# Chunk attention and a token mixer on one core: quarter-array transposes, a shared PSUM ring and an end ordered by hand

## The chip, the cores and the metric

One NeuronCore of a Trainium2 chip runs the kernel. The metric is the device time of one execution in microseconds. The kernel before has a median of 155.53 us over 3 runs (155.32 to 157.15).

## What is computed

q, k and v are float32 of shape (8 batches, 8 heads, 576 rows, 64). Attention runs inside chunks of 64 rows, then the heads are laid side by side to x of shape (8, 576, 512), and a token mixer follows:

```python
# attention, per batch, head and chunk of 64 rows
scores = q_c @ k_c.T / 8
attn   = softmax(scores)
x      = attn @ v_c                      # then (B, S, H*D) = (8, 576, 512)
# token mixer, per batch
wq, wk = x @ w_q, x @ w_k                # 576 x 64 each
W_tok  = wq @ wk.T / 8                   # 576 x 576, never formed in the kernel
out    = relu(W_tok @ x) @ w_out         # 576 x 512
```

The kernel computes `wq @ (wk.T @ x)`: the 64x512 product in the middle is its `g`.

## The kernel before

**Attention** is cut into 36 units (NU), each of 16 chunks; a batch is 4.5 units. One unit passes through these steps:

- `stage_a1`: TensorE transposes q and k, 16 transposes per unit. Each takes 128 rows by 64 columns of `qn` as weights and the 128x128 identity as moving operand, and writes 64 partitions by 128 columns of `tp` (one PSUM bank, one buffer). The array is split into two halves of 64 columns.
- `stage_a2`: VectorE copies all of `tp` (128x1024, float16) to `qkt` in SBUF.
- `stage_b1`: 16 products of 64x64 give the scores `sp`, VectorE takes the row maximum `mx`.
- `stage_b2`: VectorE subtracts (`sh`), ScalarE exponentiates (`es`).
- `stage_c`: four 128x128 transposes of `es` into `ep`, which has a PSUM bank of its own; ScalarE copies it to `et`.
- `stage_d1`, `stage_d2`: 16 products of 64x65 with v (a column of ones gives the denominator) into `xp` (two banks), then on VectorE `den`, `rec` and the normalised `x_nat`.

**The mixer** of a batch is a chain of steps, each with PSUM tiles from one ring of three banks (`m_psum`, tag "m"): `p_xt` (three times: six transposes `tx`, copy to `xt`), `p_wqk` in two halves (`wpa` of 512 and `wpb` of 64 columns, accumulated over four weights; copies to `wqkT`; then a VectorE copy of its lower 64 partitions to the upper 64 of `wqd`, line 178), `p_wkn` (18 transposes of 64x64), `p_g`, `p_mixed` twice and `p_mixed_tail` (products `ma` and `mb`, relu on ScalarE to `rmx` and `rt`), then four `p_out` (four 512-column products into `op`, copy to `osb`, store) and for each pair of batches a `p_out_tail`. A batch takes 17.5 tiles of the ring: 3 `tx`, 2 for `p_wqk`, `wknp`, `gp`, 4 `ma`, 2 `mb`, 4.5 for the outputs.

**The order** is written by hand: every engine executes its instructions in the order in which the Python code issues them. The loop over `kk` issues, per iteration: `stage_b1(kk)`, `stage_d1(kk-2)`, the mixer steps planned for place 0, `stage_a1(kk+2)`, `stage_c(kk-1)`, `stage_b2(kk)`, `stage_d2(kk-2)`, `stage_a2(kk+2)`, then the mixer steps of place 2 and as many `p_out` as a budget allows. So VectorE's order per unit is `mx`, `sh`, `den`, `rec`, `x_nat`, `qkt`; TensorE's is `sp`, `xp`, a mixer step, `tp`, `ep`, then `tx`, `wpa`/`wpb` or `op`. What is left after the loop is merged by a rule with estimated costs (lines 514 to 527). Loads are issued by GpSimd, output stores by SyncE.

Of the kernel before, what the change touches and what calls it, by code (L numbers as in the profile page):

```python
# [17 lines left out]
def kernel(  # L18
# [15 lines left out]
    nc = tc.nc  # L34
# [10 lines left out]
    NU = B * NI // 8  # L45
    R, G = 2, 32
# [12 lines left out]
    osb_pool = ctx.enter_context(tc.tile_pool(name="osb", bufs=4))  # L59

    PS = bass.MemoryType.PSUM
    t_psum = ctx.enter_context(tc.tile_pool(name="tps", bufs=1, space=PS))
    s_psum = ctx.enter_context(tc.tile_pool(name="sps", bufs=1, space=PS))
    et_psum = ctx.enter_context(tc.tile_pool(name="etps", bufs=1, space=PS))
    x_psum = ctx.enter_context(tc.tile_pool(name="xps", bufs=1, space=PS))
# [60 lines left out]

    def relu(on_vector, to, of):
        if on_vector:
            nc.vector.tensor_scalar(to, of, scale_moe, 0.0, op0=ALU.mult, op1=ALU.max)
        else:  # L130
            nc.scalar.activation(to, of, AF.Relu, scale=scale_moe)  # L131
# [3 lines left out]
    def make_moe(b):  # L135
        st = sts[b]

        def p_xt(g):
            def run():
                if g == 0:  # L140
                    st["xt"] = xt_pool.tile([P, NI, CH], F16, name="xt", tag="xt")
                xt = st["xt"].rearrange("p (s two) c -> p s (two c)", two=2)
                tx = m_psum.tile([P, 6, P], F16, name="tx", tag="m")
                for j in range(6):
                    nc.tensor.transpose(  # L145
                        tx[:, j, :], x_nat[:, b * NS + 6 * g + j, :, :], ident[:]
                    )
                if b == B - 1 and g == 2:
                    nc.vector.tensor_copy(xt[:, 12:15, :], tx[:, 0:3])
                    nc.scalar.copy(xt[:, 15:18, :], tx[:, 3:6])  # L150
                else:
                    nc.scalar.copy(xt[:, 6 * g : 6 * g + 6, :], tx[:])  # L152

            return run

        def p_wqk(half):
            def run():
                xt = st["xt"]
                if half == 0:
                    st["pa"] = m_psum.tile([P, 512], F32, name="wpa", tag="m")  # L160
                    st["pb"] = m_psum.tile([P, CH], F32, name="wpb", tag="m")
                pa, pb = st["pa"], st["pb"]
                for i in (2 * half, 2 * half + 1):
                    flags = dict(start=(i == 0), stop=(i == HQ - 1))
                    nc.tensor.matmul(
                        pa[:, :], lhsT=wqk16[:, i, :], rhs=xt[:, NC_ * i : NC_ * i + 8, :], **flags
                    )
                    nc.tensor.matmul(
                        pb[:, :], lhsT=wqk16[:, i, :], rhs=xt[:, NC_ * i + 8, :], **flags
                    )  # L170
                if half == 0:
                    return
                wqkT = moe_pool.tile([P, S], F16, name="wqkT", tag="wqkT")
                wqd = moe_pool.tile([P, S], F16, name="wqd", tag="wqd")
                nc.scalar.copy(wqkT[:, 0:512], pa[:])
                (nc.vector.tensor_copy if b == B - 1 else nc.scalar.copy)(wqkT[:, 512:S], pb[:])

                nc.vector.tensor_copy(wqd[CH:P, :], wqkT[0:CH, :])
                st["wqkT"], st["wqd"] = wqkT, wqd

            return run

        def p_wkn():


            wk = st["wqkT"][CH:P]
            wp = m_psum.tile([P, NC_, DH], F16, name="wknp", tag="m")
            for n in range(NC_):
                for o in range(2):
                    nc.tensor.transpose(  # L190
                        wp[CH * o : CH * o + CH, n, :],
                        wk[:, ds((2 * n + o) % NC_ * CH, CH)],
                        ident[CH:P, CH:P],
                    )
            wkn = moe_pool.tile([P, NC_, DH], F16, name="wkn", tag="wkn")
            nc.scalar.copy(wkn[:], wp[:])
            st["wkn"] = wkn

        def p_g():


            wkn = st["wkn"]
            gp = m_psum.tile([P, 2, P], F32, name="gp", tag="m")
# [29 lines left out]
        def p_mixed(w):  # L233
            def run():
                if w == 0:
                    st["rmx"] = moe_pool.tile([P, HQ, 512], F16, name="rmx", tag="rmx")
                ms = [m_psum.tile([P, 512], F32, name=f"ma{par}", tag="m") for par in range(2)]
                mix(ms, w, slice(0, 512))
                for par in range(2):

                    relu(
                        b == B - 1 and par == 1,
                        st["rmx"][:, 2 * w + par].rearrange("p (c g r) -> p c g r", g=G, r=R),
                        ms[par][:].rearrange("p (c r g) -> p c g r", g=G, r=R),
                    )

            return run

        def p_mixed_tail():
# [5 lines left out]
            mb = [m_psum.tile([P, 2, CH], F32, name=f"mb{par}", tag="m") for par in range(2)]  # L255
# [3 lines left out]
            for par in range(2):  # L259
                relu(  # L260
                    b == B - 1 and par == 1,
# [4 lines left out]
        def p_out(t):  # L266
            def run():
                rmx = st["rmx"]
                op = m_psum.tile([P, DM], F32, name="op", tag="m")
# [8 lines left out]
                osb = osb_pool.tile([P, DM], F32, name="osb", tag="osb")  # L278
                if b == B - 1 and t == 3:

                    hw = DM // 2
                    nc.scalar.copy(osb[:, 0:hw], op[:, 0:hw])
                    nc.vector.tensor_copy(osb[:, hw:], op[:, hw:])
                    nc.scalar.dma_start(out[b, ds(t * P, P), 0:hw], osb[:, 0:hw])
                    nc.sync.dma_start(out[b, ds(t * P, P), hw:], osb[:, hw:])
                    return
                (nc.vector.tensor_copy if b == B - 1 and t % 2 else nc.scalar.copy)(osb[:], op[:])  # L287
# [4 lines left out]
        def p_out_tail():  # L292

            rt = st["rt"]
            op = m_psum.tile([P, DM], F32, name="opt", tag="m")
# [9 lines left out]
            nc.scalar.copy(osb[:], op[:])  # L305
# [26 lines left out]
    def stage_a1(u):  # L332

        tp = t_psum.tile([P, 2, 2, 4, R, G], F16, name="tp", tag="tp")
        for j in range(2):
            b, t = batch_of(2 * u + j)
            for ti in range(2):
                part = t >= cuts[1][0]
                src = data[b, part, ti][:, :, t - cuts[part][0]]
                for r in range(R):  # L340
                    for sl in range(2):
                        nc.tensor.transpose(  # L342
                            tp[CH * sl : CH * sl + CH, j, ti, :, r, :],
                            src[:, sl, r * D : r * D + D],
                            ident[:],
                        )
        state[u] = {"tp": tp}

    def stage_a2(u):
# [3 lines left out]
            qkt[:].rearrange("p j t c k -> p (j t c k)"),  # L353
            tp[:].rearrange("p j t c r g -> p (j t c r g)"),
# [37 lines left out]
    def stage_c(u):  # L392
        es = state[u]["es"]
        ep = et_psum.tile([P, 4, P], F16, name="ep", tag="ep")
# [97 lines left out]
    for kk in range(NU + 2):  # L492
        if kk < NU:
            stage_b1(kk)
# [7 lines left out]
        if 1 <= kk <= NU:  # L502
            stage_c(kk - 1)
        if kk < NU:
            stage_b2(kk)
# [8 lines left out]
    rest = [x for key in sorted(plan) for x in plan[key]]  # L514
    last = [x for x in rest if x[0] == B - 1]
    rest = [x for x in rest if x[0] < B - 1]
    clock, due = 0.0, 0.0
    while last or rest or outs:
        if last and (clock >= due + last[0][2] or not (rest or outs)):
            entry = last.pop(0)  # L520
            clock = due = max(clock, due) + run(entry)
        elif rest:
            clock += run(rest.pop(0))
        else:
            _, cost, step = outs.pop(0)
            step()
            clock += cost
# [28 lines left out]
```

## Time and profile before

| | |
|---|---|
| median of 3 runs | 155.53 us |
| the profiled execution's own time | 156.93 us |
| its span, first to last instruction | 155.0 us |
| VectorE in 20 to 40 us, 40 to 60, 60 to 80, 80 to 100 | 18.86, 19.18, 18.43, 18.73 us busy of 20 |
| TensorE in the same stretches | 15.90, 17.72, 19.25, 19.52 us |
| ScalarE in the same stretches | 11.17, 16.20, 17.43, 17.62 us |
| GpSimd's last load issued | at 103.2 us |
| last `sp` starts, last TensorE product ends | 121.43 us, about 150.0 us |

An execution's own time holds the span and about 1.9 us around it. In a row of a group of instructions, the number before the bar's second part is the sum of their durations and the mean of one; because products follow each other in a pipeline, a mean duration is longer than the distance between two starts, and it is the distance that sets a stretch's length. "busy" of TensorE counts the modelled ends, so a busy engine may still stand and wait for a bank.

### The profile page before, as it was taken

How to read it: one execution, taken by the hardware profiler on the slowest of the kernel's cores; microseconds unless marked ns; L12 is line 12 of the kernel's file. 1: busy time of each engine (PE TensorE's matmuls, PEld its weight loads, DVE VectorE, ACT ScalarE, POOL GpSimd, SP SyncE). 2: the span in 40 equal slices, each digit the busy share in tenths (PEclk: the TensorE clock that was granted, in tenths of full speed). 3: DMA queues.
4: the chain of work that ended last, by engine and by line, in shares of the span. 5: the costliest groups of instructions: out<-in, count | busy, mean ns of one | idle time of the engine just before them, and what ended most of it. 6: DMA issues, size and time to landing. Idle time of an engine off the chain costs nothing.

```text
span 155.0 us, 6022 instructions
## 1 busy us (share of the span) xinstructions
PE 129.1 (83%) x2576; PEld 84.1 (54%) x2576; DVE 111.3 (72%) x231; ACT 105.9 (68%) x208; POOL 94.4 (61%) x140
## 2 busy tenths in 40 slices
PE   0266989759588999999999999999999898898870
PEld 0145768557465666666567467565666453442320
DVE  0056799999999999998989999989897942013020
ACT  3004144656589889886997998699889998556430
POOL 8999999999799799688789988880000000000000
PEclk9999999999999999999999999999999999699997
DMA  2999999999999999999999999999224315035383
GB/s 23 146 156 164 155 167 166 111 135 156 165 167 175 164 174 174 212 211 209 196 229 182 206 211 225 193 241 219 50 72 97 117 65 189 33 111 144 139 268 136
DMA packets 82570, 24.64 MB, mean 159 GB/s; under 512 B 77296, under 2 KB 78064, under 8 KB 82544
## 3 DMA queue, kind: packets, MB, share of 16 engines
q0 software_dynamic: 77152, 14.82, 114.6%
q1 hardware_dynamic: 5248, 9.31, 17.4%
q8 instruction: 20, 0.33, 0.8%
q10 hardware_dynamic: 144, 0.13, 0.3%
q14 instruction: 6, 0.05, 0.1%
HBM read 29.62 MB, written 9.44 MB: 252 GB/s over the span
## 4 chain that ended last, share of the span: by engine, by line
PE 45%; DVE 22%; ACT 19%; issue 5%; DMA 4%; POOL 2%; SPq 1%; ACTq 0%; DVEq 0%; POOLq 0%
PE op L271 12%; PE tp L342 6%; ACT rmx L131 6%; DVE qkt L352 5%; DVE sh L381 5%; DVE x_nat L427 4%; DVE mx L375 4%; ACT es L389 4%; PE sp L367 4%; PE ep L396 4%; PE ma L227 3%; PE tx L145 3%; PE gp L212 3%; DMA qn<-in_k_dram 3%; ACT osb L287 2%
## 5 line engine op out<-in xcount | busy, mean ns | idle before, releaser
L101 POOL DMA_DIRECT2D vt<-in_v_dram x48 | 38.4, 855 | 4.1 <-DMA vt<-in_v_dram 2.6
L342 PE MATMUL tp<-ident,qn 128*64 128x128 f16 x576 | 27.4, 241 | 8.2 <-DMA qn<-in_q_dram 6.1
L398 ACT COPY et<-ep 128x512 f16<-128x512 f16 x36 | 21.2, 590 | 18.9 <-PE ep L396 18.9
L271 PE MATMUL op<-wout,rmx 128*128 128x512 f16 x128 | 32.1, 383 | 1.6 <-ACT osb L287 1.3
L352 DVE COPY qkt<-tp 128x1024 f16<-128x1024 f16 x36 | 24.5, 682 | 10.0 <-PE tp L342 9.9
L389 ACT ACTIVATE es<-sh 128x512 f16<-128x512 f32 x36 | 23.0, 638 | 10.7 <-DVE sh L381 9.9
L91 POOL DMA_DIRECT2D qn<-in_k_dram x32 | 26.7, 872 | 3.9 <-DMA qn<-in_k_dram 1.5
L342 PEld LDWEIGHTS <-qn 128*64 128x64 f16 x576 | 21.5, 122 | 12.4 <-DMA qn<-in_q_dram 6.5
L91 POOL DMA_DIRECT2D qn<-in_q_dram x32 | 27.5, 907 | 0.9 <-DMA qn<-in_q_dram 0.5
L375 DVE TENSOR_REDUCE mx<-sp 128x8 f32<-128x512 f32 x36 | 24.7, 686 | 3.6 <-PE sp L367 3.4
L381 DVE TENSOR_TENSOR sh<-sp,mx 128x512 f32<-128x512 f32 x36 | 24.9, 692 | 2.3
L427 DVE TENSOR_TENSOR x_nat<-xp,rec 128x512 f16<-128x512 f32 x36 | 24.9, 692 | 1.2
L287 ACT COPY osb<-op 128x512 f32<-128x512 f32 x30 | 17.7, 594 | 6.5 <-PE op L271 2.8
L367 PEld LDWEIGHTS <-qkt 64*64 64x64 f16 x576 | 12.9, 115 | 14.3 <-issue 6.3
L367 PE MATMUL sp<-qkt 64*64 64x64 f16 x576 | 17.1, 203 | 3.4 <-DVE qkt L352 1.9
L152 ACT COPY xt<-tx 128x768 f16<-128x768 f16 x23 | 18.4, 801 | 0.1
L271 PEld LDWEIGHTS <-rmx 128*128 128x128 f16 x128 | 11.7, 98 | 12.1 <-issue 2.5
L412 PE MATMUL xp<-vt,et 64*64 64x65 f16 x576 | 13.0, 201 | 4.8 <-DVE x_nat L427 4.1
L131 ACT ACTIVATE rmx<-ma 128x512 f16<-128x512 f32 x30 | 16.4, 596 | 0.4 <-PE ma L227 0.3
L396 PE MATMUL ep<-ident,es 128*128 128x128 f16 x144 | 15.2, 232 | 0.0
L412 PEld LDWEIGHTS <-et 64*64 64x64 f16 x576 | 9.6, 111 | 6.4 <-ACT es L389 3.8
L145 PE MATMUL tx<-ident,x_nat 128*128 128x128 f16 x144 | 12.7, 227 | 0.0
(47 smaller groups left out, 144.1 us busy)
## 6 DMA issues: line engine op xcount, KB each, us to landing
out_dram<-osb SPq DMA_DIRECT2D x31, 256.0 KB, 2.8
qn<-in_q_dram POOLq DMA_DIRECT2D x16, 160.0 KB, 5.5
qn<-in_k_dram POOLq DMA_DIRECT2D x16, 160.0 KB, 6.2
qn<-in_q_dram POOLq DMA_DIRECT2D x16, 128.0 KB, 6.1
qn<-in_k_dram POOLq DMA_DIRECT2D x16, 128.0 KB, 5.5
vt<-in_v_dram POOLq DMA_DIRECT2D x8, 160.0 KB, 6.5
vt<-in_v_dram POOLq DMA_DIRECT2D x16, 80.0 KB, 5.8
out_dram<-osb SPq DMA_DIRECT2D x9, 128.0 KB, 2.4
```

The lines of the kernel that those rows point to most:

```text
L91: nc.gpsimd.dma_start(tl[:, sl], of[sl, :, t0:t1, :])
L101: nc.gpsimd.dma_start(vt[to : to + rows, sl, :, 0:D], of[sl, at : at + rows, n0:n1, :])
L131: nc.scalar.activation(to, of, AF.Relu, scale=scale_moe)
L271: nc.tensor.matmul(op[:], lhsT=rmx[:, i, ds(t * P, P)], rhs=wout16[:, i, :], start=(i == 0), stop=(i == HQ - 1),)
L342: nc.tensor.transpose(tp[CH * sl : CH * sl + CH, j, ti, :, r, :], src[:, sl, r * D : r * D + D], ident[:],)
L352: nc.vector.tensor_copy(qkt[:].rearrange("p j t c k -> p (j t c k)"), tp[:].rearrange("p j t c r g -> p (j t c r g)"),)
L367: nc.tensor.matmul(sp[rows, i ^ sl, :], lhsT=qkt[rows, j, 0, c, :], rhs=qkt[rows, j, 1, c, :], start=True, stop=True,)
L375: nc.vector.tensor_reduce(mx[:], sp[:], axis=AX.X, op=ALU.max)
L381: nc.vector.tensor_tensor(out=sh[:].rearrange("p i (g r) -> p i r g", g=G, r=R), in0=sp[:].rearrange("p i (r g) -> p i r g", g=G, r=R), in ...
L389: nc.scalar.activation(es[:], sh[:], AF.Exp, scale=scale_attn)
L412: nc.tensor.matmul(xv[CH * par : CH * par + CH, sl, m, :], lhsT=et[at : at + CH, m, CH * sl : CH * sl + CH], rhs=vt[at : at + CH, sl, 0 : ...
L427: nc.vector.tensor_tensor(out=x_nat[:, 4 * u : 4 * u + 4, :, :].rearrange("p m l d -> p l m d"), in0=xv[:, :, :, 0:D], in1=rec[:, :, :, No ...
```

## The change

1. `stage_a1`: the 128-row transposes become 64x64 blocks, 32 per unit, each in one quarter of the array: `h` chooses the rows of the source (and of the array) and also one of two PSUM banks, `sl` the columns. `tp` now has two banks, each half used. `stage_a2` copies the same 1,024 elements, read from two banks and written in runs of 128.
2. `ep` loses its own bank. A helper `bank()` gives it, and every mixer tile, a bank of the ring of three: 22 tiles per batch instead of 17.5. After the switch `drain[0] = True` two of five tiles go to the banks of `sp` and `tp`.
3. `p_wqk`: 320 and 256 columns in place of 512 and 64. Before the drain, `wqd` is filled by a transfer on SyncE's queue (6 batches) and not by VectorE.
4. The last unit and the end are written out: `stage_c` and `stage_d` of the last two units are issued earlier among the mixer steps, `p_mixed_tail` of batch 5 later; copies are shared between ScalarE and VectorE (`copy(on_vector, ...)`), the last `tx`, `wknp` and `op` are cut in two, and `osb` has 8 buffers.

```diff
-    osb_pool = ctx.enter_context(tc.tile_pool(name="osb", bufs=4))
+    osb_pool = ctx.enter_context(tc.tile_pool(name="osb", bufs=8))
...
-    et_psum = ctx.enter_context(tc.tile_pool(name="etps", bufs=1, space=PS))
...
+    def bank(shape, dtype, name):
+        taken[0] += 1
+        if drained() and taken[0] % 5 == 0:
+            return s_psum.tile(shape, dtype, name=name, tag="sp")
+        if drained() and taken[0] % 5 == 2:
+            return t_psum.tile(shape, dtype, name=name, tag="tp")
+        return m_psum.tile(shape, dtype, name=name, tag="m")
...
-                nc.vector.tensor_copy(wqd[CH:P, :], wqkT[0:CH, :])
+                if drained():
+                    nc.vector.tensor_copy(wqd[CH:P, :], wqkT[0:CH, :])
+                else:
+                    nc.sync.dma_start(wqd[CH:P, :], wqkT[0:CH, :])
...
-        tp = t_psum.tile([P, 2, 2, 4, R, G], F16, name="tp", tag="tp")
+        tp = t_psum.tile([P, 2, 2, 2, 2, 2, R * G], F16, name="tp", tag="tp")
+        tq = tp[:, :, 0]
...
                 for r in range(R):
-                    for sl in range(2):
+                    for h, sl in ((0, 0), (1, 1), (0, 1), (1, 0)):
+                        rows = slice(CH * h, CH * h + CH)
                         nc.tensor.transpose(
-                            tp[CH * sl : CH * sl + CH, j, ti, :, r, :],
-                            src[:, sl, r * D : r * D + D],
-                            ident[:],
+                            tq[CH * sl : CH * sl + CH, h, j, ti, :, r * G : r * G + G],
+                            src[rows, sl, r * D : r * D + D],
+                            ident[rows, rows],
                         )
...
         nc.vector.tensor_copy(
-            qkt[:].rearrange("p j t c k -> p (j t c k)"),
-            tp[:].rearrange("p j t c r g -> p (j t c r g)"),
+            qkt[:].rearrange("p j t (h c) k -> p h (j t) (c k)", h=2),
+            tp[:, :, 0].rearrange("p h j t c k -> p h (j t) (c k)"),
         )
...
-        ep = et_psum.tile([P, 4, P], F16, name="ep", tag="ep")
+        ep = bank([P, 4, P], F16, name="ep")
...
-    while last or rest or outs:
...
+    u = NU - 1
+    stage_b1(u)
+    stage_d1(u - 2)
+    stage_c(u - 1)
+    stage_b2(u)
+    stage_d2(u - 2)
+    drain[0], taken[0] = True, 0
...
+    put(len(outs) - 14)
+    chain(B - 2, 2)
+    stage_c(u)
+    stage_d1(u - 1)
+    stage_d2(u - 1)
+    put()
+    stage_d1(u)
+    stage_d2(u)
+    chain(B - 1)
+    chain(B - 2)
+    chain(B - 1)
+    put()
+    chain(B - 1)
+    chain(B - 3)
+    chain(B - 2)
+    put(2)
+    chain(B - 1, 2)
+    chain(B - 2, 2)
+    chain(B - 1)
+    put()
+    chain(B - 1)
+    put()
+    chain(B - 2)
+    chain(B - 1, 3)
+    put(len(outs))
```

`chain(b)` issues the next mixer step of batch b (numbered from 0, so B - 1 is 7), `put(n)` the next n outputs.

More of the change, by code (lines that the diff above doesn't have):

```diff
@@ L45 @@
     NU = B * NI // 8
+    W0 = 5 * CH
     R, G = 2, 32
@@ L58 @@
     moe_pool = ctx.enter_context(tc.tile_pool(name="moep", bufs=2))
-    osb_pool = ctx.enter_context(tc.tile_pool(name="osb", bufs=4))
+    osb_pool = ctx.enter_context(tc.tile_pool(name="osb", bufs=8))
     PS = bass.MemoryType.PSUM
+    s_psum = ctx.enter_context(tc.tile_pool(name="sps", bufs=1, space=PS))
+    x_psum = ctx.enter_context(tc.tile_pool(name="xps", bufs=1, space=PS))
     t_psum = ctx.enter_context(tc.tile_pool(name="tps", bufs=1, space=PS))
-    s_psum = ctx.enter_context(tc.tile_pool(name="sps", bufs=1, space=PS))
-    et_psum = ctx.enter_context(tc.tile_pool(name="etps", bufs=1, space=PS))
-    x_psum = ctx.enter_context(tc.tile_pool(name="xps", bufs=1, space=PS))
     m_psum = ctx.enter_context(tc.tile_pool(name="mps", bufs=3, space=PS))
@@ L125, with drained, copy @@
     load_v(1, 0)
+    drain = [False]
+    taken = [0]
+    def bank(shape, dtype, name):
[5 more added lines that the diff above has]
+        return m_psum.tile(shape, dtype, name=name, tag="m")
+    def drained():
+        return drain[0]
+    def copy(on_vector, to, of):
+        (nc.vector.tensor_copy if on_vector else nc.scalar.copy)(to, of)
     def relu(on_vector, to, of):
@@ L142, in run @@
                 xt = st["xt"].rearrange("p (s two) c -> p s (two c)", two=2)
[L143 to L152, printed above, removed]
+                halves = 2 if b == B - 1 and g == 2 else 1
+                for h in range(halves):
+                    n = 6 // halves
+                    tx = bank([P, n, P], F16, name="tx")
+                    for j in range(n):
+                        nc.tensor.transpose(
+                            tx[:, j, :], x_nat[:, b * NS + 6 * g + n * h + j, :, :], ident[:]
+                        )
+                    at = 6 * g + n * h
+                    copy(b == B - 1 and g + h == 1 or h == 1, xt[:, at : at + n, :], tx[:])
             return run
@@ L159, in run @@
                 if half == 0:
-                    st["pa"] = m_psum.tile([P, 512], F32, name="wpa", tag="m")
-                    st["pb"] = m_psum.tile([P, CH], F32, name="wpb", tag="m")
+                    st["pa"] = bank([P, W0], F32, name="wpa")
+                    st["pb"] = bank([P, S - W0], F32, name="wpb")
                 pa, pb = st["pa"], st["pb"]
@@ L164, in run @@
                     flags = dict(start=(i == 0), stop=(i == HQ - 1))
[L165 to L170, printed above, removed]
+                    for to, c0, c1 in ((pa, 0, W0 // CH), (pb, W0 // CH, NC_)):
+                        nc.tensor.matmul(
+                            to[:],
+                            lhsT=wqk16[:, i, :],
+                            rhs=xt[:, NC_ * i + c0 : NC_ * i + c1, :],
+                            **flags,
+                        )
                 if half == 0:
@@ L174, in run @@
                 wqd = moe_pool.tile([P, S], F16, name="wqd", tag="wqd")
-                nc.scalar.copy(wqkT[:, 0:512], pa[:])
-                (nc.vector.tensor_copy if b == B - 1 else nc.scalar.copy)(wqkT[:, 512:S], pb[:])
-                nc.vector.tensor_copy(wqd[CH:P, :], wqkT[0:CH, :])
+                copy(False, wqkT[:, 0:W0], pa[:])
+                copy(drained(), wqkT[:, W0:S], pb[:])
+                if drained():
+                    nc.vector.tensor_copy(wqd[CH:P, :], wqkT[0:CH, :])
+                else:
+                    nc.sync.dma_start(wqd[CH:P, :], wqkT[0:CH, :])
                 st["wqkT"], st["wqd"] = wqkT, wqd
@@ L186, in p_wkn @@
             wk = st["wqkT"][CH:P]
[L187 to L194, printed above, removed]
-            wkn = moe_pool.tile([P, NC_, DH], F16, name="wkn", tag="wkn")
-            nc.scalar.copy(wkn[:], wp[:])
+            wkn = moe_pool.tile([P, NC_, DH], F16, name="wkn", tag="wkn")
+            cuts_ = (0, 5, NC_) if b == B - 1 else (0, NC_)
+            for n0, n1 in zip(cuts_, cuts_[1:]):
+                wp = bank([P, n1 - n0, DH], F16, name="wknp")
+                for n in range(n0, n1):
+                    for o in range(2):
+                        nc.tensor.transpose(
+                            wp[CH * o : CH * o + CH, n - n0, :],
+                            wk[:, ds((2 * n + o) % NC_ * CH, CH)],
+                            ident[CH:P, CH:P],
+                        )
+                copy(n0 > 0, wkn[:, n0:n1], wp[:])
             st["wkn"] = wkn
@@ L202, in p_g @@
             wkn = st["wkn"]
-            gp = m_psum.tile([P, 2, P], F32, name="gp", tag="m")
+            gp = bank([P, 2, P], F32, name="gp")
             lo, hi = slice(0, CH), slice(CH, P)
@@ L236, in run @@
                     st["rmx"] = moe_pool.tile([P, HQ, 512], F16, name="rmx", tag="rmx")
-                ms = [m_psum.tile([P, 512], F32, name=f"ma{par}", tag="m") for par in range(2)]
+                ms = [bank([P, 512], F32, name=f"ma{par}") for par in range(2)]
                 mix(ms, w, slice(0, 512))
@@ L241, in run @@
                     relu(
-                        b == B - 1 and par == 1,
+                        drained() and par == 1,
                         st["rmx"][:, 2 * w + par].rearrange("p (c g r) -> p c g r", g=G, r=R),
@@ L254, in p_mixed_tail @@
                 st["rt"] = sts[b - 1]["rt"]
-            mb = [m_psum.tile([P, 2, CH], F32, name=f"mb{par}", tag="m") for par in range(2)]
+            mb = [bank([P, 2, CH], F32, name=f"mb{par}") for par in range(2)]
             for w in range(2):
@@ L260, in p_mixed_tail @@
                 relu(
-                    b == B - 1 and par == 1,
+                    drained() and par == 1,
                     to[:, par, b % 2],
@@ L268, in run @@
                 rmx = st["rmx"]
-                op = m_psum.tile([P, DM], F32, name="op", tag="m")
+                osb = osb_pool.tile([P, DM], F32, name="osb", tag="osb")
+                if b == B - 1 and t == 3:
+                    hw = DM // 2
+                    for h, store in ((0, nc.scalar), (1, nc.sync)):
+                        cols = slice(hw * h, hw * h + hw)
+                        op = bank([P, hw], F32, name="op")
+                        for i in range(HQ):
+                            nc.tensor.matmul(
+                                op[:],
+                                lhsT=rmx[:, i, ds(t * P, P)],
+                                rhs=wout16[:, i, cols],
+                                start=(i == 0),
+                                stop=(i == HQ - 1),
+                            )
+                        copy(h == 1, osb[:, cols], op[:])
+                        store.dma_start(out[b, ds(t * P, P), cols], osb[:, cols])
+                    return
+                op = bank([P, DM], F32, name="op")
                 for i in range(HQ):
@@ L277, in run @@
                     )
[L278 to L287, printed above, removed]
+                copy(drained() and b > B - 3 and t % 2, osb[:], op[:])
                 nc.sync.dma_start(out[b, ds(t * P, P), :], osb[:])
@@ L294, in p_out_tail @@
             rt = st["rt"]
-            op = m_psum.tile([P, DM], F32, name="opt", tag="m")
+            op = bank([P, DM], F32, name="opt")
             for i in range(HQ):
@@ L304, in p_out_tail @@
             osb = osb_pool.tile([P, DM], F32, name="osb", tag="osb")
-            nc.scalar.copy(osb[:], op[:])
+            copy(b == B - 1, osb[:], op[:])
             for o in range(2):
@@ L332, in stage_a1 @@
     def stage_a1(u):
-        tp = t_psum.tile([P, 2, 2, 4, R, G], F16, name="tp", tag="tp")
+        tp = t_psum.tile([P, 2, 2, 2, 2, 2, R * G], F16, name="tp", tag="tp")
+        tq = tp[:, :, 0]
         for j in range(2):
             b, t = batch_of(2 * u + j)
+            part = t >= cuts[1][0]
             for ti in range(2):
-                part = t >= cuts[1][0]
                 src = data[b, part, ti][:, :, t - cuts[part][0]]
                 for r in range(R):
-                    for sl in range(2):
+                    for h, sl in ((0, 0), (1, 1), (0, 1), (1, 0)):
+                        rows = slice(CH * h, CH * h + CH)
                         nc.tensor.transpose(
-                            tp[CH * sl : CH * sl + CH, j, ti, :, r, :],
-                            src[:, sl, r * D : r * D + D],
-                            ident[:],
+                            tq[CH * sl : CH * sl + CH, h, j, ti, :, r * G : r * G + G],
+                            src[rows, sl, r * D : r * D + D],
+                            ident[rows, rows],
                         )
@@ L491 @@
     stage_a(0)
-    for kk in range(NU + 2):
-        if kk < NU:
-            stage_b1(kk)
+    for kk in range(NU - 1):
+        stage_b1(kk)
         if kk >= 2:
@@ L501 @@
             reload(load_qk, kk + 2, 2, NT, cuts)
-        if 1 <= kk <= NU:
+        if kk >= 1:
             stage_c(kk - 1)
-        if kk < NU:
-            stage_b2(kk)
+        stage_b2(kk)
         if kk >= 2:
@@ L512, with chain, put @@
         fill(kk, 2, 1.4 if len(outs) < 4 else 1.9)
[L514 to L517, printed above, removed]
-    while last or rest or outs:
[L519 to L527, printed above, removed]
+    left = {}
+    for key in sorted(plan):
+        for b, *_, step in plan[key]:
+            left.setdefault(b, []).append(step)
+    assert [len(left[b]) for b in sorted(left)] == [1, 7, 10]
+    def chain(b, n=1):
+        for _ in range(n):
+            left[b].pop(0)()
+    def put(n=1):
+        for _ in range(n):
+            outs.pop(0)[2]()
+    u = NU - 1
[5 more added lines that the diff above has]
+    drain[0], taken[0] = True, 0
+    for b in range(B - 3, B):
+        outs.extend(moes[b][2])
+    put(len(outs) - 14)
[23 more added lines that the diff above has]
+    put(len(outs))
 _INS = ['q', 'k', 'v', 'moe_w_q', 'moe_w_k', 'moe_w_out']
```

## The prediction

> **What bounds the kernel now.** I began with the page's 40 slices: rows of busy tenths, one digit per 3.9 us.
>
> ```profile
> PE   0266989759588999999999999999999898898870
> DVE  0056799999999999998989999989897942013020
> ACT  3004144656589889886997998699889998556430
> PEclk9999999999999999999999999999999999699997
> ```
>
> There are three parts: a start up to about 10 us, a stretch in which VectorE (DVE) is full while TensorE (PE) fills up behind it, and from slice 31 (121 us) an end in which VectorE is nearly idle. PEclk has one dip, near 134 us.
>
> The chain of waits tells what a unit costs where VectorE alone binds:
>
> ```profile
> 24.74 0.69 DVE x_nat L427
> 25.43 0.60 DVE qkt L352
> 26.03 0.61 DVE mx L375
> 26.73 0.69 DVE sh L381
> ...
> 27.77 0.69 DVE x_nat L427
> ...
> 37.54 0.60 DVE qkt L352
> 38.17 0.50 DVE wqd L178
> 38.70 0.70 DVE mx L375
> ```
>
> From `x_nat` to `x_nat` is 3.03 us (2.96 where `mx` starts without its small gap). No unit can be shorter unless VectorE's own work shrinks. Where `wqd` stands between `qkt` and `mx`, those two are 1.16 us apart and not 0.60: `wqd` costs the chain 0.56 us.
>
> From the `mx` at 35.0 us to the one at 121.9 us there are 27 units in 86.9 us, 3.22 each. At 2.96 they would take 79.9 us, so 7.0 us lie above the floor. Up to six `wqd` copies explain 3.4 us. The rest is VectorE waiting for TensorE; the list of waits and groups gives:
>
> ```profile
> DVE mx L375 <- PE sp L367: 3.4, 7, 0.7
> ACT et L398 <- PE ep L396: 18.9, 22, 3.7
> L352 DVE COPY qkt<-tp 128x1024 f16<-128x1024 f16 x36 | 24.5, 682 | 10.0 <-PE tp L342 9.9
> L381 DVE TENSOR_TENSOR sh<-sp,mx 128x512 f32<-128x512 f32 x36 | 24.9, 692 | 2.3
> ```
>
> **Part 1, the quarters.** The timeline has one unit's transposes in the middle, and in another unit the only work that already uses all four quarters:
>
> ```profile
> 87.37 0.64 PE L342 MATMUL tp<-ident,qn 128*64 128x128 f16 x16
> 87.94 0.40 PE L396 MATMUL ep<-ident,es 128*128 128x128 f16 x4
> ```
>
> ```profile
> 102.33 0.32 PE L412 MATMUL xp<-vt,et 64*64 64x65 f16 x16
> ```
>
> A merged row is as long as 15 starts plus one duration. `tp`: (0.64 - 0.22)/15 = 28 ns per start, 16 x 28 = 0.45 us, and `ep` starts 0.57 us after `tp`, so 0.12 us pass at the change of array form. `xp`: (0.32 - 0.19)/15 = 8.5 ns per start. At that rate 32 quarter transposes take 0.27 us, 0.18 less. `wknp` (64x64) is followed by `tp` (128x64) 0.40 us after its start; 18 starts at 16.4 ns make 0.30 of it. So 0.10 us go to the change of form, which falls away wherever `tp` follows 64x64 work, and comes back only after `gp`: in about 3 of 4.5 units net, 0.07 us each. TensorE saves 0.18 + 0.07 = 0.25 us per unit. The dearer bound is the rate of `sp` and `wknp`, which use two blocks at a time, 16.4 ns: 32 x 16.4 = 0.52 us, 0.07 more than now, cancelled by the forms. I take 8.5 ns, because `xp` has the same block size and the same spread over quarters.
>
> The Trainium skill speaks against this step. "TensorE: Matmul & The Clock Gate", section "Wait — 56ns, not 53.3ns?", says that the distance between starts never falls below about 25 ns, however small the product. By that, 32 transposes would take an estimated 0.80 us and each unit would lose 0.35 us. The `xp` row at 8.5 ns shows that quarters overlap; a floor of that kind can hold only inside one quarter, and the row decides.
>
> What this is worth: before 35 us VectorE's chain hides it, save where `tp` itself is on the chain, at units 0, 2 and 3 (1.01 and 1.08 us at 13.4 and 15.2 us). There starts lie 50 ns apart, and those of `xp` 13, so about 0.8 becomes 0.4; after the last load only part of unit 0 is left. I take 0.6 us in all (0 to 1.2). In the middle, a saving reaches the end only where `mx` waits for `sp`: 3.4 us in 7 waits. These come in runs of two or three heavy units, so some 8 units give 8 x 0.25 = 2.0 us (0 to 3.4).
>
> **The copy of `tp`.** It still moves 1,024 float16 values, now in runs of 128 from two banks. 682 ns for 1,024 against 692 for 512 in `sh` shows two values per step. If the broken pattern kept that, it costs nothing; if it lost it, twice `sh` less one fixed part of about 0.15 us is 1.23 us, 0.55 more per unit. No row has such a pattern. I take nothing, because innermost runs stay contiguous and even. "VectorE: DVE Perf Modes", section "What auto-detection actually checks", names 16-bit data at step 1 as the condition, which agrees; no run here shows it yet.
>
> **Part 2, the shared ring.** `ep` used to find its bank free. Now it takes the bank used three tiles earlier. In the unit at 86 to 88 us that would be the `op` copied by ScalarE at 86.87 (0.60 long), free at 87.47; `ep` came at 87.94, or about 87.7 when TensorE is quicker: 0.2 us to spare. The `op` after it would need the first relu of a pair that runs from 87.47 to 88.56: just in time. So the ring is at its edge. What is queued behind a waiting `ep` is everything on TensorE, next `tx` or `op`, then `sp` for which `mx` waits. Bounds: nothing, or one ScalarE copy (0.59) in each of 27 units, 16 us. I take 0.03 us per unit, 0.8 us, by this row, which is nearest to zero.
>
> **Part 3, `wqd` by a transfer.** VectorE loses six copies of 0.56 us of chain. Where VectorE waits for TensorE anyway one is worth less, so I count five: 2.8 us (1.4 to 3.4). On SyncE's queue the six transfers stand after stores whose `osb` copies ScalarE finishes earlier anyway, so they block nothing. The smaller stores take 2.4 us to land; the first product that reads `wqd` comes three units, 9 us, later, and that cover hides them. If the cover were gone, each would cost 2.4 us less the 0.5 of the old copy, about 12 us in all. The split 320/256 moves columns between two ScalarE copies and leaves their sum.
>
> **Part 4, the end.** From the last `sp` (121.43 us) to the last product (150.0) TensorE needs 28.5 us. Its work there: 15 output groups of 0.86 (four products of 215 ns) = 12.9; two `p_wqk` of 0.98; 3 `tx` of 0.34; 2 `wknp` of 0.3; 2 `gp` of 0.63; `ma` and `mb` 1.25; `ep`, `xp`, `sp` 1.15; about 20 changes of form at 0.1 = 2.0. Sum 22.1. So 6.4 us are waits and the half clock:
>
> ```profile
> 130.00:140.00 10.00, 8.85 (x73) 4.22 (x69) 0.89 (x3) 6.54 (x14) 0.00 (x0) 0.83 0.22 79
> ```
>
> ```profile
> 134.61 0.36 DVE L149 COPY xt<-tx 128x384 f16<-128x384 f16 x1 [5.67 <-PE tx L145]
> ```
>
> The clock of 0.83 over 10 us is 3.4 us at one half, 1.7 us lost. VectorE finished the last `x_nat` at 128.9 and then sat 5.67 us, because the last `tx` stood behind seven other pieces on TensorE. In the new order only `wknp`, two `tx` and an output lie between the last `xp` and that `tx`; the last `xp` itself moves ahead of `mb`, `wknp` and a `tx`. The same chain of batch 7 then has outputs and batch 6's products between its steps, and five banks and two copying engines to drain them. I leave 2 us of waits (the last `x_nat` before the last `tx`; the closing `ma`/`mb`, eight tiles over five banks). The end falls from 28.5 to 24.1: 4.4 us (2 to 6). The 5 us after the last product (copy, transfer, closing) stay. What is late next is TensorE itself, with eight outputs in a row.
>
> **Sum.** -0.6 - 2.0 + 0.8 - 2.8 - 4.4 = -9.0 us. The profiled execution's 156.93 us would become 147.9. That execution lay 1.4 above the median of the runs shown, so for the median I predict 155.53 - 9.0 = 146.5 us. With the terms' own bounds the likeliest case runs from 143.0 to 149.5.
>
> **Rivals.**
> - *The ring takes the middle back.* Every wait that the quarters and `wqd` save comes back as a wait of TensorE for ScalarE, whose middle is 17.5 us busy of 20. For it: ScalarE is nearly full, and the edge worked out above. Against it: ScalarE itself stood 18.9 us waiting for `ep`, which now comes sooner. Only start and end remain: 155.5 - 5.0 = 150.5 (149.5 to 152.5).
> - *The quarters do not overlap*, as transposes run in pairs only: TensorE gains nothing, and the ring's wait adds 0.1 to 0.2 us per unit over 27 units (3 to 5 us). 155.5 - 2.8 - 4.4 + 4 = 152.3 (151 to 157).
> - *The `qkt` copy loses its two values per step.* This ends slower. VectorE's floor rises by 0.55 in 36 units, 20 us; with the gains of end and `wqd` it is 155.5 + 20 - 8 = 167. It decides from 0.25 us more per copy (930 ns) on, where it eats the whole gain, and above 1,020 ns the kernel is over 2% slower. For it: no row shows the pattern. Against it: contiguous runs.
>
> **How the numbers follow.** Forecast 0.66; ring 0.17; quarters in pairs 0.09; `qkt` 0.06; 0.02 for something else on the slow side. 2% of 155.53 is 3.1 us, about what a measurement of this kernel can tell from no change: faster ends at 152.4, slower begins at 158.6. Faster: 0.66 + 0.16 + half of the pairs = 0.86; slower 0.07; the same 0.07. A range from 143.0 to 152.4 holds the forecast, the ring and a little of the pairs, 0.85, less what falls below 143.
>
> **What would show it.** Quarters: `tp` rows with starts near 8.5 ns, and 0.40 us or less from `tp` to `ep`. Copy: `qkt` still near 680 ns. Ring: few waits of `ep` for ScalarE copies; `mx` to `mx` in the middle near 3.0 to 3.1. `wqd`: no such rows on VectorE before 121 us, and no `ma` waiting for a transfer. End: no half clock near 134, the last `tx` within 8 us after the last `sp` (12.6 now), 24 us from the last `sp` to the last product. I am wrong if `qkt` is above 800 ns, or if `ep` waits in most units.

## The result and the profile after

The changed kernel takes 165.0 us (median of 4 runs, 164.82 to 165.58) against 156.13 us for the kernel before, measured beside it: ratio 1.057, 95% interval 1.049 to 1.065. It is slower; forecast were 146.5 us and a gain. Some executions of most kernels here are a few per cent longer than the rest, so ratios, here and below, are formed without those and need not equal the quotient of the medians.

The page of the changed kernel, the rows of 40 slices (4.1 us each):

```profile
PE   0237868695977998664999899996999998998980
DVE  0067998998767888973188979997789978534540
ACT  3012228356358979781389979993998997675330
PEclk9999999759557999996599999999999999999999
```

VectorE, full from slice 5 on before, now has holes, the deepest in slices 18 and 19 (73 to 81 us). The clock dips three times in the first half, and no longer at the end.

Three instants split both profiled spans: the fourth `mx` (unit 3), the last `mx` (unit 35), and the span's end.

| stretch, us | before | changed | difference | predicted |
|---|---|---|---|---|
| to the `mx` of unit 3 | 19.88 | 18.99 | -0.9 | -0.6 |
| from there to the last `mx` | 102.04 | 114.88 | +12.8 | -4.0 |
| from there to the end | 33.13 | 29.11 | -4.0 | -4.4 |

So start and end came out near what was predicted, and the whole miss lies in the middle. From the changed kernel's list of waits (us in total, times, longest) and from its groups (busy us, mean ns of one):

```profile
DVE mx L414 <- PE sp L406: 14.4, 19, 3.8
PEld L381 <- issue: 11.2, 18, 3.5
PE tp L381 <- issue: 8.2, 5, 3.4
```

```profile
L391 DVE COPY qkt<-tp 128x1024 f16<-128x1024 f16 x36 | 24.5, 682 | 12.0 <-PE tp L381 12.0
```

`mx` waits 14.4 us for `sp` (3.4 before). The copy of `tp` stayed at 682 ns, so that rival is out. The quarters themselves are as fast as predicted where nothing disturbs them; the timeline of a unit at 124.8 us:

```profile
124.83 0.45 PE L381 MATMUL tp<-ident,qn 64*64 64x64 f16 x32
125.21 0.40 PE L435 MATMUL ep<-ident,es 128*128 128x128 f16 x4
```

`ep` follows `tp` after 0.38 us (0.57 before): (0.45 - 0.20)/31 = 8 ns per start. What is new are stops in which TensorE waits for nothing that the profile shows. The longest, in TensorE's timeline and then in VectorE's (in brackets: the idle time before the row, and what ended it):

```profile
71.81 0.25 PE L381 MATMUL tp<-ident,qn 64*64 64x64 f16 x3
75.46 0.58 PE L381 MATMUL tp<-ident,qn 64*64 64x64 f16 x26 [3.40 <-issue]
```

```profile
76.08 0.69 DVE L391 COPY qkt<-tp 128x1024 f16<-128x1024 f16 x1 [2.09 <-PE tp L381]
80.61 0.69 DVE L414 TENSOR_REDUCE mx<-sp 128x8 f32<-128x512 f32 x1 [3.83 <-PE sp L406]
```

In the middle of 32 transposes on data long loaded, TensorE does nothing for 3.4 us. Counting its weight loads and products in the order of the trace, the stops over 0.45 us without a wait in the instruction stand at numbers 1462, 1972, 2226, 2482, 2738, 2994, 3760 and 4784: all a multiple of 256 apart, to within 6. (Two more gaps, 0.69 and 0.94 us before numbers 444 and 716, are waits for data: TensorE goes on 0.04 us after a load of k lands.) The page lists the transfers that bring instructions:

```profile
q8 instruction: 24, 0.39, 1.0%
```

That is 24 pieces of 16 KB; stops 256 instructions apart make it 64 bytes for each. Before there were 20, and a single such stop, 0.60 us, in a weight load of `gp` (number 2478). From the page and the list of waits of before:

```profile
q8 instruction: 20, 0.33, 0.8%
PEld L212 <- issue: 0.8, 2, 0.6
```

The eight stops of the changed kernel, gaps between starts, add up to 12.1 us.

### The profile page after: what moved, and what is told of

Read it like the earlier page. It is cut to its first block, busy times and chain, and to the rows that moved or that the text cites. A ratio compares the mean times of both kernels' runs of the same rounds, so it can differ in the third digit from the quotient of the medians.

```text
span 163.0 us, 7181 instructions
## 1 busy us (share of the span) xinstructions
PE 127.3 (78%) x3156; PEld 84.8 (52%) x3156; DVE 114.7 (70%) x235; ACT 102.4 (63%) x199; POOL 94.7 (58%) x140
## 4 chain that ended last, share of the span: by engine, by line
PE 51%; POOL 12%; ACT 11%; DVE 9%; issue 8%; DMA 7%; DVEq 0%; ACTq 0%; POOLq 0%
PE op L316 16%; POOL qn L92 8%; PE tx L168 4%; PE tp L381 4%; PE ep L435 4%; PE sp L406 4%; ACT rmx L150 4%; DMA qn<-in_k_dram 3%; POOL vt L102 3%; DMA vt<-in_v_dram 3%; PE xp L451 3%; PE ma L254 3%; PE gp L239 3%; PE wpa L186 2%; PE opt L333 2%
## 5 line engine op out<-in xcount | busy, mean ns | idle before, releaser
L381 PE MATMUL tp<-ident,qn 64*64 64x64 f16 x1152 | 23.5, 212 | 17.9 <-issue 8.2
L414 DVE TENSOR_REDUCE mx<-sp 128x8 f32<-128x512 f32 x36 | 24.8, 688 | 14.7 <-PE sp L406 14.4
L316 PE MATMUL op<-wout,rmx 128*128 128x512 f16 x124 | 32.3, 395 | 0.2
L381 PEld LDWEIGHTS <-qn 64*64 64x64 f16 x1152 | 19.5, 123 | 20.9 <-issue 11.2
L144 ACT COPY osb<-op 128x512 f32<-128x512 f32 (+1 forms) x29 | 16.9, 588 | 8.8 <-PE op L316 6.5
L406 PEld LDWEIGHTS <-qkt 64*64 64x64 f16 x576 | 14.0, 122 | 14.7 <-issue 10.1
L406 PE MATMUL sp<-qkt 64*64 64x64 f16 x576 | 18.3, 210 | 3.5 <-DVE qkt L391 2.5
L451 PE MATMUL xp<-vt,et 64*64 64x65 f16 x576 | 14.7, 209 | 5.6 <-issue 1.6
L144 ACT COPY xt<-tx 128x768 f16<-128x768 f16 (+1 forms) x23 | 18.1, 788 | 1.0 <-PE tx L168 0.9
L435 PE MATMUL ep<-ident,es 128*128 128x128 f16 x144 | 16.6, 248 | 0.0
L150 ACT ACTIVATE rmx<-ma 128x512 f16<-128x512 f32 x28 | 15.2, 599 | 1.5 <-PE ma L254 1.4
L168 PE MATMUL tx<-ident,x_nat 128*128 128x128 f16 x144 | 13.7, 236 | 1.4 <-issue 0.8
```

Of the source, the lines that this page charges most:

```text
L144: (nc.vector.tensor_copy if on_vector else nc.scalar.copy)(to, of)
L316: nc.tensor.matmul(op[:], lhsT=rmx[:, i, ds(t * P, P)], rhs=wout16[:, i, :], start=(i == 0), stop=(i == HQ - 1),)
L381: nc.tensor.transpose(tq[CH * sl : CH * sl + CH, h, j, ti, :, r * G : r * G + G], src[rows, sl, r * D : r * D + D], ident[rows, rows],)
L406: nc.tensor.matmul(sp[rows, i ^ sl, :], lhsT=qkt[rows, j, 0, c, :], rhs=qkt[rows, j, 1, c, :], start=True, stop=True,)
L414: nc.vector.tensor_reduce(mx[:], sp[:], axis=AX.X, op=ALU.max)
L435: nc.tensor.transpose(ep[:, m, :], es[:, 2 * m : 2 * m + 2, :], ident[:])
```

## The experiments

The theory to test (A): TensorE's program is fetched in pieces of 256 instructions while the loads fill the transfer engines, and the quarters, 64 instructions per unit where there were 32, use pieces up faster than they come. The rivals: the halved clock (B) and the shared ring (C).

**e1, the quarters undone.**

```diff
-        tp = t_psum.tile([P, 2, 2, 2, 2, 2, R * G], F16, name="tp", tag="tp")
+        tp = t_psum.tile([P, 2, 2, 4, R, G], F16, name="tp", tag="tp")
...
-                    for h, sl in ((0, 0), (1, 1), (0, 1), (1, 0)):
+                    for sl in range(2):
```

> The changed kernel with stage_a1 and stage_a2 as before (16 transposes of 128 rows per unit, one bank for tp); ring of three, wqd by a transfer and the new end stay. Theory A (instructions): in the changed kernel TensorE stops where its instruction stream runs dry; its records show stops 256 instructions apart, and the quarters raise its program from some 5,150 to 6,310 instructions. Then this kernel, with 5,162, loses the stops: 146 to 149 us. Theory B (clock): the shorter transposes leave TensorE too idle and the clock is halved; this kernel would be as fast, 147 to 150 us, with a mean granted clock near 0.98. Theory C (ring): ep waits for ScalarE's copies in the shared ring; the time stays near 163 to 165 us.

Measured: 155.76 us beside 157.57 for before (ratio 0.999, 0.994 to 1.004). The large stops are gone, and with them some 9 us; but no theory's range holds 155.8. Stops of 0.5 to 1.2 us are left, and TensorE waits for ScalarE in the ring. Its timeline:

```profile
48.59 0.38 PE L433 MATMUL ep<-ident,es 128*128 128x128 f16 x4
49.09 0.30 PE L186 MATMUL wpa<-xt,wqk 128*128 128x320 f16 x1
49.58 0.27 PE L186 MATMUL wpb<-xt,wqk 128*128 128x256 f16 x1 [0.19 <-ACT rmx L150]
```

Not `ep` waits but `wpa` and `wpb` behind it: `ep` took the third bank, and they need the other two, which the relus `rmx` still read (the trace names `rmx` for `wpb`). Without such waits `wpa` follows the start of `ep` in 0.23 us and `wpb` follows `wpa` in 0.14; here it is 0.50 and 0.49. A distance of 0.44 us or more from `wpa` to `wpb` occurs in 4 of e1's 32 pairs, one of them on a boundary.

**e2, quarters and ring put into the kernel before**, nothing else.

> The kernel before with the quarter transposes and ep in the ring of three alone; old wqd copy, old end. Theory A: the stops cost the middle 12 us as in the changed kernel and the end gains nothing: 165 to 170 us. Theory B: the same. If the loss came from the new end or the wqd transfer, this would be at 152 to 157 us.

Measured: 168.2 us (166.8 to 170.6) beside 157.57. The quarters with the ring do all the damage; new end and `wqd` transfer are cleared. Six stops stand at the same numbers (1462, 1972, 2738, 2994, 3760, 4784).

**e3 and e4, instructions or time?** Both are e1 with idle work in a free bank, after the products of `stage_d1`:

```diff
+            for x in range(16):                    # e3
+                rows = slice(CH * (x % 2), CH * (x % 2) + CH)
+                nc.tensor.matmul(dp[rows, ds(x // 2 * CH, CH)], lhsT=ident[rows, rows],
+                                 rhs=wide[rows, ds(x // 2 * CH, CH)], start=True, stop=True)
...
+            for x in range(2):                     # e4
+                rows = slice(CH * x, CH * x + CH)
+                nc.tensor.matmul(dp[rows, :], lhsT=ident[rows, rows], rhs=wide[rows, :],
+                                 start=True, stop=True)
```

> e1 plus, in stage_d1 of the first 33 units, 16 products of 64x64 into the bank that e1 leaves free; nothing reads them, and the output stays. TensorE's program has 6,218 instructions, nearly the changed kernel's, and TensorE is busier by about 0.27 us per unit. Theory A: the stops come back, 156 to 163 us. Theory B: TensorE is busier, the clock stays full, and the time is e1 plus at most 4 us for the added work. Theory C: as e1.

> e1 plus, in the same places, 2 products of 64x512 side by side: about 0.22 us of TensorE's time per unit as in e3, but only 4 instructions each instead of 32 (5,294 in all). Theory A: no stops, within 0 to 3 us of e1 and at least 7 us under e3. Theory B and C: the same time as e3.

Measured side by side: e3 166.6 us (ratio to before 1.056, 1.041 to 1.071), e4 157.7 us (1.006, 0.999 to 1.012). The added work takes about the same TensorE time (0.25 and 0.22 us from the first `dp` to the next `ma`), and yet the ratios are 0.050 apart, some 8 us. e3 is even slower than the range expected from theory A. The waits of e3 show the stops now inside the added products:

```profile
PE dp L464 <- issue: 4.6, 3, 2.7
```

They stand at 446, 700, 1462, 2482, 2738, 2994, 3250, 3760 and on, the boundaries of the changed kernel or a multiple of 256 from them, to within 8, with other work around them. e3 has no quarters and its clock is at one half for 6.8 us in all, not 23.9, and is as slow as the changed kernel. That rules out B as the main cause, and nothing about quarters as such is needed.

**e5, e6, e7: what the other parts are worth with halves.** e5 is e1 with `ep` in its own bank; e6 is e1 with four banks in the ring; e7 is e5 with `wqd` copied by VectorE, so the new end without that transfer (and with the 320 and 256 columns).

```diff
-        ep = bank([P, 4, P], F16, name="ep")                            # e5, e7
+        ep = et_psum.tile([P, 4, P], F16, name="ep", tag="ep")
...
-    m_psum = ctx.enter_context(tc.tile_pool(name="mps", bufs=3, space=PS))  # e6
+    m_psum = ctx.enter_context(tc.tile_pool(name="mps", bufs=4, space=PS))
...
-                if drained():                                           # e7
-                    nc.vector.tensor_copy(wqd[CH:P, :], wqkT[0:CH, :])
-                else:
-                    nc.sync.dma_start(wqd[CH:P, :], wqkT[0:CH, :])
+                nc.vector.tensor_copy(wqd[CH:P, :], wqkT[0:CH, :])
```

> e1 with ep back in its own bank: the kernel before with wqd by a transfer and the new end alone. e1 came out at 155.8 us where 147 was expected without stops; its time up to the last mx is 4.6 us longer than before's, its end 4.0 shorter. If the ring costs this (wpa, wpb and ma now take banks that ScalarE still reads): 147 to 149.5 us, with mx to mx mostly 2.96 to 3.3. If it is the wqd transfers, or stops of the instruction stream that remain with 5,160 instructions: 152 to 156 us.

> e1 with the ring widened to four banks, ep still in it. Ring theory: most of its cost goes, 147.5 to 151 us. Rival (transfers or stops): 153 to 156 us, as e1.

> The kernel before with the new end alone: halves, ep in its own bank, wqd copied by VectorE. The end is worth 4.0 us in the changed kernel and in e1: 150.5 to 152.5 us. If the wqd transfer is a gain as predicted (2.8), e5 is 2 to 3.5 us faster than this; if it is a loss, slower.

Measured beside a before of 158.39 us: e5 154.39 (ratio 0.978, 0.970 to 0.986), e6 154.18 (0.974, 0.964 to 0.984), e7 155.11 (152.28 to 157.99, expected 150.5 to 152.5; ratio 0.967, 0.954 to 0.979). All three beat both kernels; their order among themselves is not resolved, so no gain or loss of the `wqd` transfer is shown. Both e5 and e6 are better than e1, by 0.02 in the ratio (some 3 us) but only by 1.4 to 1.6 us in the medians, because the before beside e1 was faster (157.57). Both times lie in the range that was expected if something other than the ring remained, and e5's profile does still have stops of 1.48 and 1.00 us. So with the loads running the ring of three costs 1 to 3 us, and how much of that is stops is not separated.

**e8 to e12, the loads taken away.** In all five, loads of q, k and v after batch 1 are left out, and later batches compute on the data of batches 0 and 1:

```diff
     def load_qk(b, part):
+        if b > 1:
+            for ti in range(2):
+                data[b, part, ti] = data[b - 2, part, ti]
+            return
...
     def load_v(b, part):
+        if b > 1:
+            data[b, part, 2] = data[b - 2, part, 2]
+            return
```

> The changed kernel with no q, k and v loads after batch 1: batches 2 to 7 compute on the data of batches 0 and 1, so the output is not the reference's, with all other work in place. If pieces of TensorE's program wait behind the loads on the transfer engines: stops over 0.45 us vanish after about 35 us, and the time is 150 to 157 us (the ring stays). If the fetch itself is too slow for the program, or the clock is the cause: the stops stay at the same instructions, 160 us or more.

> The kernel before with no q, k and v loads after batch 1 (batches 2 to 7 compute on the data of batches 0 and 1; the output is not the reference's). Control to e8 (151.2 us). If loads delay the instruction stream of before too, hidden in its 155 to 159 us: 150 to 154 us, no stop over 0.45 us after 40 us. If before hardly suffers: 154.5 to 156 us.

> e1 with no loads after batch 1, as in e8: the changed kernel without the quarters and without the loads. If quarters are a gain where the instruction stream does not run dry, as the prediction has it (0.25 us per unit where mx waits for sp, 0.9 at the start): 1 to 4 us slower than e8, 152 to 155 us. If they are none: 150.5 to 152 us.

> e5 with no loads after batch 1. Against e10 it prices the ring of three without stops: 2 to 4 us under e10 if the ring costs what e1 against e5 showed (about 3 us), within 1 us if those 3 us were stops too.

> e8 plus six 128x128 transposes of the identity into the unused half of tp in each of units 0 to 11; nothing reads them. In e8 the clock fell to one half at 32.3 us for 6.8 us and two units took 3.54 and 4.39 us instead of 3.03. If too little work on TensorE halves the clock: the clock stays full from about 29 us on and those units are near 3.03, 1 to 2 us less in all. If the clock falls all the same: no change or slower by up to 1 us.

One run each, so that differences of about 1 us between them are not resolved:

| | kernel | with loads, us | without, us |
|---|---|---|---|
| e8 | changed | 165.0 | 151.23 |
| e12 | changed, clock kept up | - | 150.47 |
| e9 | before | 156.1 to 159.1 | 153.83 |
| e10 | halves, ring of three (e1) | 155.76 | 152.20 |
| e11 | halves, own bank (e5) | 154.39 | 152.23 |

The changed kernel, the slowest with loads, is the fastest without. It still fetches 24 pieces, but its last stop over 0.45 us ends at 34.6 us, 2 us after the last load landed, and the waits say:

```profile
DVE mx L421 <- PE sp L413: 3.3, 7, 0.7
```

Its units in the middle take 3.02 to 3.07 us, save two per pair of batches at 3.25 and 3.35. What changed is when a piece starts. I took each start of the next 16 KB transfer after TensorE crossed one of the boundaries, from 40 to 82 us (medians): 3.9 us after the crossing in the changed kernel, 3.0 in the one before, 0.7 in e8. The transfer takes about 1.0 us in the first two and 1.3 in e8, and in all eight stops TensorE went on 1.1 to 1.7 us after a transfer's end. So a piece is there about 6.2 us after the crossing in the changed kernel, 5.3 before, 3.3 without loads. And it must last: 256 instructions are 1.46 units in the changed kernel (6,312 instructions over 36 units), 4.4 us at 3.02 us per unit; before (5,152) they are 1.79 units, 5.7 us at the average of 3.19. The need is met by 0.4 us before, missed by 1.8 us in the change, and met by 1.1 us without loads. These margins are estimates from medians; the single starts, in the first two, spread over about 2 us or more. That a piece queues behind the loads' packets is inferred from e8; the queue itself no view shows. Leaving loads out also spares transfers and descriptors, and the kernel before gained 2.3 to 5.2 us by it, so that not all of the 13.8 us between 165.0 and 151.23 need be stops.

**The clock.** In e8 it fell to one half once before the last product; in e12, with idle transposes in the unused half of `tp`, it did not:

```diff
         tq = tp[:, :, 0]
+        spare = tp[:, :, 1].rearrange("p h j t c k -> p h (j t c k)")
+        for x in range(6 if u < 12 else 0):
+            nc.tensor.transpose(spare[:, x % 2, ds(x // 2 * P, P)], ident[:], ident[:])
```

```profile
32.30:39.10 6.80, 5.55 (x112) 4.19 (x113) 5.07 (x11) 4.00 (x8) 0.00 (x0) 0.50 0.02 5
```

```profile
32.30:39.10 6.80, 5.96 (x202) 4.92 (x202) 6.46 (x14) 3.78 (x8) 0.00 (x0) 1.00 0.03 7
```

These are the same 6.8 us in e8 and in e12 (length, busy us and instructions of PE, PEld, DVE, ACT and POOL, then the granted clock, the share of the DMA engines and GB/s): clock 0.50 and 1.00, with VectorE busy 5.07 and 6.46 us. The two long units of e8 (3.54 and 4.39) become 3.03 and 3.06, and the run is 0.8 us shorter, a little less than the 1 to 2 us expected. One stop of e8 (1.37 us at 34.6) lies in that stretch too, so the clock's share is at most the 1.9 us of those two units.

## Why the prediction was wrong

**The failed step is Part 1, "The quarters".** It priced 32 transposes by the distance of their starts, and that was right (8 ns, 0.38 us from `tp` to `ep`; no 25 ns floor). It costed the 32 added instructions per unit at nothing and gave no reason. What it left out is the fetch of the program: an estimated 0.4 us of slack per piece in the kernel before, already visible as the 0.60 us stop and its row "<- issue", which I passed over. In its place the runs showed eight stops of 12.1 us in all, in a middle that is 12.8 us longer. e3 against e4 shows the price of the instructions alone, some 8 us with the time they take held nearly equal; the changed kernel with loads against e8 agrees. No rival named it, and the range excluded it.

The Trainium skill has the mechanism, in "Runtime: NRT & Kernel Launch", section "Instruction fetch mechanics": programs come in blocks of 16 KiB, 256 instructions, and the cost of crossing a block is "mostly hidden". The block size agrees with the stops 256 apart. "Mostly hidden" does not: up to 3.4 us of one crossing were bare here.

**The other terms, one by one.**
- *Start*, -0.6: measured -0.9 between the profiles, -0.5 between e8 and e9. Right.
- *Saving where `mx` waits*, -2.0: hidden by the stops. Without loads and at full clock, e12 against e10 (same ring) takes 98.6 us and not 101.2 from the fourth to the last `mx`, 2.5 us less, of which a wait of e10 for a load of k (0.61 us at 24 us) is part. Size about right, by one run each and under conditions that the change itself does not reach.
- *The copy of `tp`*, 0: 682 ns, right.
- *The ring*, +0.8: with loads 1 to 3 us (e1 against e5 and e6), stops included; without loads nothing in the total (e10 and e11, 152.20 and 152.23) as was expected of e11 if the cost with loads were stops too, and 1.2 us in the middle, half of it the wait for k just named. Inside the bounds, but in the wrong place: I asked only whether `ep` finds its bank, not who comes after it. The wait that the trace shows is at `wpa` and `wpb`.
- *`wqd` by a transfer*, -2.8: mis-sized. From the fourth to the last `mx`, e11 takes 99.96 us and e9 100.22, 0.3 us less. A unit without the copy takes 3.02 to 3.03 us; before, the units beside a copy ran at 2.96, so the copy took the place of small gaps in the chain as well as lengthening it. I had multiplied one row, 0.56 us, by five.
- *The end*, -4.4: -4.0 between the profiles. Of this the half clock is up to 1.7: it came 11 us after the last `mx` in before (133 us) and in e2 (143 us), both with the old end, but not in e9. Without loads e9 ends 31.8 us after its last `mx` and e8 29.4, 2.4 less. In the changed kernel the last `tx` starts 7.4 us after the last `sp` (133.4 to 140.8), as predicted under 8, and the last product ends 25.0 us after that `sp`, near the predicted 24.

So even with the stops taken away the change is worth 2.6 to 3.4 us (e8 and e12 against e9) and not 9. In e12 against e9 the middle is 1.6 us shorter where 4.0 were forecast, mostly because of the `wqd` term, and the end 2.6 where 4.4 were.

**A base that moved.** The profile of before shows one stop; its median beside later experiments was 157.6 and 158.4 us. e7, which before the end is nearly the same program, shows stops of 1.94, 0.75, 0.71 and 1.73 us in its profiled execution, a multiple of 256 instructions apart to within 13, the second of them at the number of before's stop. With so little slack the kernel before would sometimes pay too; that this moved its median is not shown.

## What to carry to other kernels

Price an edit on TensorE in instructions as well as in array time: divide 256 by the instructions per period, multiply by the period, and compare that with how long the next piece takes to arrive while the loads run (an estimated 5 to 6 us here). Splitting work into smaller tiles that run side by side is a gain of array time and a loss of program length; in this kernel the first was worth 1 to 2 us in all (e8 and e12 against e10, single runs) and the second cost 8 to 9 (e3 against e4, the changed kernel against e1). When one tile more enters a ring of buffers, look at the tiles after it, not only at the one that moved.

## What the runs showed of the hardware

- TensorE stopped for up to 3.6 us between two starts, in the middle of a row of independent transposes, at places a multiple of 256 instructions apart. The views call this "issue", a name that also covers harmless idle times of weight loads while products run: 20 in the kernel before at `ma` and `mb`, line 227, 0.37 us on average and at most 0.6.
- Four quarters of the array together start a 64x64 transpose every 8 ns, as they do products of 64x65 (8.5 ns).
- TensorE can lose its clock in the middle of the work. The first drop in the changed kernel, at 30.4 us, came after a window without a stop:

```profile
27.00:30.40 3.40, 1.91 (x77) 1.35 (x77) 3.19 (x9) 2.40 (x5) 3.40 (x6) 1.00 1.69 111
```

  TensorE was busy 1.91 of 3.40 us there; the kernel before, with 2.51 in the same window, kept the clock. But in the window 28.9 to 32.3 e8, with 2.06, lost the clock and e12, with 1.96, kept it, so the busy share alone does not decide, and what does stays open. The stretches at one half in the changed kernel last 6.8, 10.2 and 6.8 us, multiples of 3.4.
